# Two weighted sums at a time, and the feed-forward's token sums and second plain unit moved into the end of the attention

## The chip, the cores and the metric

The kernel runs on one core of a Trainium2 chip. The metric is the time of one execution in device microseconds (us). Engines are named as in the profile: PE multiplies matrices, DVE does vector arithmetic, ACT activations, casts and copies, POOL the rest of the vector work, SP issues most transfers. PSUM, the memory that PE writes, has eight banks of 512 fp32 values per partition.

## What is computed

One transformer block on 2048 tokens of width 640, in fp32:

```python
h  = x + attention(layernorm(x)) @ wo          # 32 heads of 20, a token sees itself and 255 before it
h2 = h + (gelu(n @ w_gate) * (n @ w_up)) @ w_down   # n = layernorm(h), inner width 1536
```

## The kernel before

**Numbers.** Each fp32 operand of the dense products is held as two fp16 halves, high and low; a product is three matmuls (high with high, high with low, low with high). A split is a cast on ACT and a subtraction on DVE.

**Attention.** The tokens are 16 blocks of 128. A block has eight units of four heads; a unit looks at up to three blocks of keys. For each unit there are a maximum (`maxima`: products on PE, masking and reduction on DVE in `max_out`), the scores (`scores`: products again with the maximum folded in, the exponential on ACT and masking on POOL in `score_out`, result in a buffer `pt` of which there are three), and the weighted sum (`value_lane`: 12 matmuls `ps<-pt,v` into a bank, copied by ACT to `oT` in `value_out`). `row_lane` issues maxima and scores two units at a time, one in each of two sets of three banks; below, such a group of 24 matmuls is a ROW, and 12 matmuls of a weighted sum are a VAL. A ROW can start when the two sets are free: one waits for DVE's reduction, the other for ACT's exponential. After four units `normalise` transposes `oT` and divides; after eight, `o_transpose` splits the block and turns it through transposing DMAs (or, for the last block, on PE), and `wo_block` multiplies it with `wo` (weights w3h, w3l). Keys lie in a ring `kT` of three slots of two blocks. Key and query projections (`qk`, weights w0 and w1) and values (`vproj`, w2) are dense products that the lane `dense_lane` hands out 15 matmuls at a time between the ROWs.

**Feed-forward.** The tokens are four chunks of 512, the inner width three groups of 512; a unit (chunk, group) is a `gate_up`, then a `down` of 96 matmuls (DN). Units go in the order `SEQ` (L1165): (0,0), (1,0), (0,1), (1,1), ... Units (0,0) and (1,0) have a plain `gate_up` (L1364): 120 matmuls of 512 columns in eight groups of 15 (PLAIN). All others use a scheme with fewer products (`gate_up_sums`, L1228: twice 108 matmuls of 256 columns, SUMS), which needs sums of token blocks (`token_sums`, L1317: ten additions and four splits per chunk, tiles tTh and tTl) and sums of weight blocks (class `Sums`, L488; `sums`, L524: four additions into a tile `sums`, of which one is in use at a time). Weights come through a ring of three stage slices `wsl`: once for their scale (`scale`: ACT squares each slice, a matmul with `dg` on PE makes the maximum known to all partitions) and once for the split.

**The order of work.** Everything is written by generators ("lanes"). A clock inside the kernel estimates when each engine is free and each operand ready, and a loop at the end (L1680 on) takes the first lane of a list that may start: ready outputs first, then transposes, side work, and PE's three lanes. Each engine's program is thus a fixed queue, and an instruction behind a waiting one waits too.

**Around the change.** When the projections are used up, `dense_lane` (L1548) opens the pool `ffb` and fills its turns with `first_feed_forward` (L1608): PLAIN and DN of unit (0,0). When all blocks are out it closes the attention's pools, opens `ffp` in their room and goes on with (1,0). The token sums of chunks 0 and 1, the second loading of the group-1 weights and the splits of these weights all follow that opening.

Of the kernel before, what the change touches and what calls it, by code (L numbers as in the profile page):

```python
# [23 lines left out]
P = 128  # L24
# [240 lines left out]
def block_kernel(ctx: ExitStack, tc: tile.TileContext, x, wqkv, wo, wg, wu, wd, out):  # L265
# [115 lines left out]
    class Weight:  # L381
# [19 lines left out]
        def load(self, room):  # L401
            self.sliced = False
            for i in range(self.shape[0]):
# [4 lines left out]
        def load_slices(self, turn):  # L408
            self.sliced = True
            for i in self.order if turn else range(self.shape[0]):  # L410
# [75 lines left out]
    class Sums(Weight):  # L486
# [3 lines left out]
        N = 17  # L490

# [21 lines left out]
        def rest(self, hi, lo, src, sc, name, i):  # L513
# [3 lines left out]
            opened["sums"] -= name[0] in ("S", "EE")  # L517
            if i is not None:
                self.left[i] -= 1
                if not self.left[i]:  # L520
                    for _ in range(2 if i < 2 else 1):
                        self.done_with()
# [13 lines left out]
        def split(self, hl):  # L536
            self.hl = hl
            self.left, self.tm = {0: 3, 1: 3, 2: 2}, {}
# [11 lines left out]
            yield on("vector", e, when=lambda: opened["sums"] < 1)  # L550
            t = nc.tile(ffp, [P, 4, 256], F32, "sums")
            opened["sums"] += 1
            nc.vector.tensor_tensor(t[:, 0], e[:, :256], e[:, 256:], op=ALU.subtract)
            yield from self.take(16, t[:, 0], ("EE", 0), 2)
# [156 lines left out]
    kT = wp.tile([P, RK // 2, H // 2, CW], F16, name="kT")  # L711
# [373 lines left out]

    def value_out(j, u, ps):
        b = B[j]
        yield on("scalar", ps[:, 0:P], when=lambda: u == 0 or b.kept == u)
        if u % 4 == 0:
            b.oT = at("oT", [P, 4, P], F32, 1)  # L1090
        nc.scalar.copy(b.oT[:, u % 4, :], ps[:, 0:P])
        done(ps)
        b.kept = u + 1
        if u % 4 == 3:
            tps.append(normalise(j, u // 4, b.oT))

    def normalise(j, half, oT):
# [6 lines left out]
        for u4 in range(4):  # L1104
            nc.tensor.transpose(t[:, u4 * P:u4 * P + OR], oT[:OR, u4, :], ident[:OR, :OR])
        tv = t.rearrange("p (h e) -> p h e", e=32)
# [60 lines left out]
    POOL = (0, 1, 1, 0)  # L1167
    ffpools = [None, None]
# [21 lines left out]
    def gate_out(c, fg, ft, pss):  # L1190

        i = SEQ.index((c, fg)) % 2
# [34 lines left out]

    def gate_up_sums(c, fg):  # L1228
        i = SEQ.index((c, fg)) % 2
# [3 lines left out]
        ah = nc.tile(ffpools[i], [P, FT, CB * P], F16, "ah")  # L1233
        al = nc.tile(ffpools[i], [P, FT, CB * P], F16, "al")
# [82 lines left out]
    def token_sums(c):  # L1317

        yield on("vector", when=lambda: ffpools[1] and chunk[c] == CB
                 and (c == 0 or ("T", c - 1) in flags))  # L1320
        pool = ffpools[1 - POOL[c]]
        tT[c] = tuple(nc.tile(pool, [P, 8, 256], F16, n) for n in ("tTh", "tTl"))
# [5 lines left out]
        x = nc.tile(ffp, [P, 4, 256], F32, "tsum")  # L1328
# [431 lines left out]
```

## Time and profile before

| what | value |
| --- | --- |
| median of 3 runs (lowest, highest) | 1029.72 us (1029.27, 1033.44) |
| the profiled execution: its time, its span | 1026.79 us, 1025.1 us |
| busy, share of the span | PE 94%, DVE 71%, ACT 47%, POOL 23% |
| mean granted clock of PE | 0.99 |
| chain that ended last, by engine | PE 72%, DMA 9%, DVE 8%, ACT 4%, issue 4%, POOL 2% |

The span runs from the first to the last instruction of the profiled execution. A row of the timeline gives start, duration, engine, operation and count; a bracket at its end gives the idle time of the engine just before it and what ended it. Nearly all rows have line L211, a helper through which every instruction is issued, so places are found by tile names and time. A VAL's 12 matmuls are fp32 and leave 24 records. Pieces overlap on PE, so the length of one is taken from its start to the start of the next. A row of the table of stretches gives the stretch and its length, busy time and count of PE, PEld (PE's weight load), DVE, ACT and POOL, then PE's granted clock, the DMA engines' busy share and GB/s.

### The profile page before, as it was taken

The page shows a single profiled execution, that of the slowest core. Times are in us where ns is not written, and L with a number is a line of the kernel's source. Part 1 is how long each engine was busy: PE and PEld are TensorE (multiplying, and loading weights), DVE is VectorE, ACT ScalarE, POOL GpSimd, SP SyncE. Part 2 cuts the span into 40 slices and gives each one's busy share as a digit, 9 for nine tenths or more (in the row PEclk, how much of TensorE's full clock was granted, in tenths as well). Part 3 has the DMA queues.
Part 4 walks back from the last instruction along what each step waited for, and adds up shares of the span by engine and source line. Part 5 has one row for each costly group of instructions (what it writes and reads, how often), then busy time and mean ns, then how long its engine had stood idle before and what let it go on. Part 6 is the DMA issues. An engine that isn't in the chain of part 4 may idle for free.

```text
span 1025.1 us, 27364 instructions
## 1 busy us (share of the span) xinstructions
PE 960.0 (94%) x11687; PEld 730.9 (71%) x11687; DVE 732.6 (71%) x1393; ACT 478.6 (47%) x769; POOL 240.4 (23%) x336
## 2 busy tenths in 40 slices
PE   3997898999899999998989889989999999999998
PEld 2885675767677867776556655878888888888886
DVE  6978886767866656666878338979978869764563
ACT  6635664555556655555665635453522224231120
POOL 5202233544434333333334420000121100000000
PEclk9999999999999999999989999999999999999999
DMA  8447675463463613517474214252443322100002
GB/s 333 124 126 208 176 186 127 92 130 85 88 148 76 138 47 92 106 40 206 137 163 80 41 42 143 80 155 78 110 98 100 94 91 72 40 14 1 1 1 103
DMA packets 109306, 106.90 MB, mean 104 GB/s; under 512 B 59136, under 2 KB 79872, under 8 KB 107264
## 3 DMA queue, kind: packets, MB, share of 16 engines
q1 hardware_dynamic: 86080, 94.40, 35.1%
q10 hardware_dynamic: 23104, 10.75, 4.1%
q8 instruction: 91, 1.49, 0.6%
q14 instruction: 31, 0.25, 0.1%
HBM read 71.11 MB, written 20.97 MB: 90 GB/s over the span
## 4 chain that ended last, share of the span: by engine, by line
PE 72%; DMA 9%; DVE 8%; ACT 4%; issue 4%; POOL 2%; ACTq 1%; SPq 0%; DVEq 0%; POOLq 0%
PE ps L211 72%; DMA ol<-spl 2%; DMA xt<-in_x_dram 2%; ACT pt L211 2%; DMA qk<-qks 2%; DVE mxs L211 1%; DMA wsl<-in_wd_dram 1%; DVE gel L211 1%; DMA h0l<-spl 1%; POOL pt L211 1%; POOL spl L211 1%; ACTq L211 1%; DVE ps L211 1%; DVE tsum L211 1%; ACT wsl L211 1%
## 5 line engine op out<-in xcount | busy, mean ns | idle before, releaser
L211 ACT ACTIVATE pt<-ps,esc 128x1536 f32<-128x1536 f32 (+2 forms) x128 | 186.4, 1460 | 97.8 <-PE ps L211 87.9
L211 POOL TENSOR_SCALAR_AFFINE_SELECT pt<-pt 128x512 f32<-128x512 f32 x240 | 151.4, 653 | 265.8 <-ACT pt L211 265.6
L211 DVE TENSOR_REDUCE mxs<-ps 128x4 f32<-128x1024 f32 (+1 forms) x128 | 151.4, 1186 | 2.7
L211 DVE TENSOR_TENSOR gel<-gel,ps 128x512 f32<-128x512 f32 x140 | 93.9, 683 | 52.7 <-PE ps L211 52.2
L211 DVE COPY_PREDICATED ps<-mask,ps 128x512 f32<-128x512 int32 x112 | 77.4, 692 | 64.2 <-PE ps L211 63.6
L211 PEld LDWEIGHTS <-wu 128*128 128x128 f16 x1080 | 105.7, 98 | 12.2
L211 PEld LDWEIGHTS <-gu 128*128 128x128 f16 x888 | 86.6, 98 | 36.4 <-issue 2.9
L211 PE MATMUL ps<-pt,v 128*21 128x128 f32 x2880 | 106.0, 277 | 5.9 <-ACT pt L211 2.5
L211 PE MATMUL ps<-qT,kT 62*128 62x128 f16 x1440 | 101.1, 219 | 5.1 <-ACT pt L211 2.4
L211 PEld LDWEIGHTS <-qT 60*128 60x128 f16 x1440 | 80.3, 94 | 35.2 <-issue 34.9
L211 PE MATMUL ps<-kT,qT 60*128 60x128 f16 x1440 | 102.7, 218 | 2.6 <-DVE mxs L211 1.8
L211 PEld LDWEIGHTS <-ah 128*128 128x128 f16 x768 | 74.7, 98 | 31.3 <-issue 3.1
L211 PEld LDWEIGHTS ps<-pt,v 128*21 128x21 f32 x2880 | 68.2, 101 | 26.3 <-POOL pt L211 5.2
L211 DVE SCALAR_TENSOR_TENSOR ht<-ps,ffk,ht 128x320 f32<-128x320 f32 x96 | 52.1, 546 | 43.7 <-PE ps L211 43.2
L211 PEld LDWEIGHTS <-kT 62*128 62x128 f16 x1440 | 78.7, 95 | 6.1 <-issue 5.2
L211 PE MATMUL ps<-wdh,ah 128*128 128x320 f16 x256 | 76.6, 299 | 2.1 <-ACT oT L211 1.4
L211 PE MATMUL ps<-wdh,al 128*128 128x320 f16 x256 | 76.5, 299 | 0.0
L211 PE MATMUL ps<-wdl,ah 128*128 128x320 f16 x256 | 76.5, 299 | 0.0
L211 ACT CAST ah<-gel 128x512 f16<-128x512 f32 x48 | 29.6, 617 | 95.6 <-DVE gel L211 95.5
L211 PE MATMUL ps<-xh,w0h 128*128 128x256 f16 x200 | 55.7, 279 | 8.8 <-ACT w0h L211 5.4
L211 PE MATMUL ps<-tTh,wu 128*128 128x256 f16 x320 | 60.6, 273 | 0.0
L211 PE MATMUL ps<-xh,w1h 128*128 128x256 f16 x200 | 54.5, 274 | 4.0 <-ACT oT L211 3.4
(219 smaller groups left out, 2273.8 us busy)
## 6 DMA issues: line engine op xcount, KB each, us to landing
wsl<-in_wd_dram SPq DMA_DIRECT2D x28, 320.0 KB
qk<-qks ACTq DMA_DIRECT2D x64, 128.0 KB
wsl<-in_wg_dram SPq DMA_DIRECT2D x30, 256.0 KB
wsl<-in_wu_dram SPq DMA_DIRECT2D x30, 256.0 KB
qT<-qk SPq DMA_DIRECT2D x16, 320.0 KB
kT<-qk SPq DMA_DIRECT2D x16, 320.0 KB
ht<-in_x_dram SPq DMA_DIRECT2D x16, 320.0 KB
h_dram<-ht SPq DMA_DIRECT2D x16, 320.0 KB
```

Source lines behind the costliest of these rows:

```text
L211: r = real(*args, **kw)
```

## The change

1. The weighted sums take two units at once: `value_lane` waits until two units are in its queue and issues their 24 matmuls back to back into one bank, and `value_out` copies both with one ACT copy.
2. The plain `gate_up` of unit (1,0) is issued inside the attention, behind unit (0,0). Its gelu is the tanh-approximation activation, where (0,0) builds its own from tanh. What follows the attention is the DN of (1,0), then SUMS of (0,1) and (1,1).
3. The token sums of chunks 1 and 0 are issued inside the attention too, with the x tiles as room for intermediates; the attention ends only when those of chunk 0 are done. Chunk 0's result lies in the third slot of the key ring, which moves to a pool that outlives the attention.
4. The second slot of that ring gives two buffers for sums (`KSUM`, handed out by `sum_room`), the first one the activations of every other unit (`act_room`).
5. Three slices of the group-1 gate weights are loaded again before the attention ends; the other two, and those of the up weights, after it. Chunk 1's `ht` tiles are loaded right at the end of the attention.
6. The loop's list of outputs puts `max_out` and `score_out` ahead of other outputs.

```diff
         def sums(self, k):
+            yield on("vector", when=lambda: idle_sums and (1, k) in self.raw
+                     and (1, k + 2) in self.raw)
             a, b = self.raw[1, k], self.raw[1, k + 2]
             a1, a2, b1, b2 = a[:, :256], a[:, 256:], b[:, :256], b[:, 256:]
-            yield on("vector", a, b, when=lambda: opened["sums"] < 1)
-            t = nc.tile(ffp, [P, 4, 256], F32, "sums")
-            opened["sums"] += 1
+            yield on("vector", a, b, when=lambda: idle_sums)
+            t, _ = sum_room(self, ("S", k))
...
-                tasks.append(self.sums(k))
+                tasks.append(self.sums(1) if not k else self.end_sum())
...
-    kT = wp.tile([P, RK // 2, H // 2, CW], F16, name="kT")
+    kT = ffw.tile([P, RK // 2, H // 2, CW], F16, name="kT")
+    kparts = [kT[:, i, 8 * k:8 * k + 8, :] for i in range(3) for k in range(2)]
+    KAH, KSUM, KTOK = 0, 2, 4
+    idle_sums = [KSUM, KSUM + 1]
+
+    def sum_room(w=None, name=None):
+        i = idle_sums.pop(0)
+        if w:
+            w.at_[name] = i
+        return kparts[i].bitcast(F32).rearrange("p (a b) n -> p a (b n)", b=2), i
...
-            yield pe(when=lambda: valq and B[valq[0][0]].v == 2 and pos["ones"])
-            j, u = valq.popleft()
+            yield pe(when=lambda: len(valq) > 1 and B[valq[0][0]].v == 2 and pos["ones"])
+            units = sorted(valq.popleft() for _ in range(2))
+            j = units[0][0]
             b = B[j]
-            pt = b.pt.pop(u)
+            pts = [b.pt.pop(u) for _, u in units]
             ks = window(j)
             n = len(ks)
             order = [1, 0, 2] if n == 3 else list(range(n))
-            yield pe(pt[:, 3 - n:3], slots=["pv"])
+            yield pe(*(pt[:, 3 - n:3] for pt in pts), slots=["pv"])
             ps = bank("pv")
-            pv = ps[:, 0:P]
-            for k, i in enumerate(order):
-                for c in range(4):
-                    nc.tensor.matmul(pv[32 * c:32 * c + DH + 1],
-                                     vring[ks[i] % RV][:, 4 * u + c, :], pt[:, 3 - n + i, c, :],
-                                     start=(k == 0), stop=(k == n - 1))
-            pos["values"] += 1
-            tasks.append(value_out(j, u, ps))
-            if u == 7:
+            for m, (_, u) in enumerate(units):
+                pv = ps[:, m * P:m * P + P]
+                for k, i in enumerate(order):
+                    for c in range(4):
+                        nc.tensor.matmul(pv[32 * c:32 * c + DH + 1],
+                                         vring[ks[i] % RV][:, 4 * u + c, :],
+                                         pts[m][:, 3 - n + i, c, :],
+                                         start=(k == 0), stop=(k == n - 1))
+                pos["values"] += 1
+            tasks.append(value_out(j, [u for _, u in units], ps))
+            if pos["values"] % (H // 4) == 0:
...
-        yield on("scalar", ps[:, 0:P], when=lambda: u == 0 or b.kept == u)
-        if u % 4 == 0:
+        yield on("scalar", ps[:, 0:2 * P], when=lambda: pos["norm"] == 2 * j + us[0] // 4)
+        if b.kept % 4 == 0:
             b.oT = at("oT", [P, 4, P], F32, 1)
-        nc.scalar.copy(b.oT[:, u % 4, :], ps[:, 0:P])
+        x, y = (u % 4 for u in us)
+        nc.scalar.copy(b.oT[:, x:y + 1:y - x, :], ps[:, 0:2 * P].rearrange("p (a q) -> p a q", q=P))
         done(ps)
-        b.kept = u + 1
-        if u % 4 == 3:
-            tps.append(normalise(j, u // 4, b.oT))
+        b.kept += 2
...
+    def act_room(i):
+        if i:
+            return [t.rearrange("p (a b) n -> p a (b n)", b=2) for t in kparts[KAH:KAH + 2]]
+        return [nc.tile(ffpools[0], [P, FT, CB * P], F16, n) for n in ("ah", "al")]
...
-        yield on("vector", when=lambda: ffpools[1] and chunk[c] == CB
-                 and (c == 0 or ("T", c - 1) in flags))
+        last = ("T", (1, None, 0, 2)[c])
+        yield on("vector", when=lambda: chunk[c] == CB and (c == 1 or last in flags)
+                 and (c or B[NB - 3].scored))
         pool = ffpools[1 - POOL[c]]
-        tT[c] = tuple(nc.tile(pool, [P, 8, 256], F16, n) for n in ("tTh", "tTl"))
+        tT[c] = (kparts[KTOK:KTOK + 2] if POOL[c] == 0 else
+                 tuple(nc.tile(pool, [P, 8, 256], F16, n) for n in ("tTh", "tTl")))
...
+        if c < 2:
+            o, q = (at("xt", [P, D], F32)[:, :512].rearrange("p (a n) -> p a n", a=2)
+                    for _ in range(2))
+        else:
+            yield on("vector", when=lambda: idle_sums)
+            x, taken = sum_room()
+            o, q = x[:, 0:2], x[:, 2:4]
...
+        yield from W["g", 1].load_slices(1, (0, 2, 1))
         yield ("sync",), need(when=lambda: ffpools[1] and W["d", 1].scaled, eng="sync")
         room = nc.tile(ffp, [P, 2, 17 * 256], F16, "wu2").bitcast(F32)
         room = room.rearrange("p a f -> p (a f)")
-        W["g", 1].load([room[:, 512 * k:512 * k + 512] for k in range(KC)])
-        W["u", 1].load([nc.tile(ffp, [P, D], F32, "ht", CB)[:, :512] if k < CB else
-                        room[:, 512 * KC:512 * KC + 512] for k in range(KC)])
+        W["g", 1].load({k: room[:, 512 * k:512 * k + 512] for k in (3, 4)})
+        W["g", 1].sliced, W["g", 1].ring = True, (0, 2, 1)
+        W["u", 1].load([room[:, 512 * (KC + k):512 * (KC + k) + 512] if k < 3 else
+                        nc.tile(ffp, [P, D], F32, "lxn", 2)[:, :512] for k in range(KC)])
...
-        while pos["h"] < NB or any(not b.wrote for b in B):
+        while pos["h"] < NB or any(not b.wrote for b in B) or ("T", 0) not in flags:
...
-                    side.extend(((LATE, chunk_lane(0)), (LATE, norm_lane(1, range(CB), "h"))))
+                    side.extend(((LATE, chunk_lane(0)), (LATE, norm_lane(1, range(CB), "h")),
+                                 (LATE, token_sums(1)), (LATE, token_sums(0))))
...
-        side.append((LATE, token_sums(0)))
+        load_h(1, ffp, CB)
         for c in range(1, NCH):
-            if c == 1:
-                side.append((LATE, after_lane(lambda: W["u", 1].ready, token_sums(1))))
-            side.append((LATE, chunk_lane(c)))
+            if c > 1:
+                side.append((LATE, chunk_lane(c)))
...
         yield from gate_up(0, 0)
         yield from down(0, 0)
+        yield from gate_up(1, 0)
 
     def feed_forward():
+        yield from down(*SEQ[1])
         prev = None
-        for c, fg in SEQ[1:]:
+        for c, fg in SEQ[2:]:
...
+        outs.sort(key=lambda l: l.gen.__name__ not in ("max_out", "score_out"))
```

PE, in the middle of the attention, before: the last matmul of a dense group, one VAL (pt is the unit's exponentials, v0 to v5 the values), the first weight load of a ROW.

```order
L211 MATMUL ps8_73<-xh_3908,w0l_219 128x256
L211 MATMUL ps8_73<-pt_5274,v0_101 21x128 x4
L211 MATMUL ps8_73<-pt_5274,v5_106 21x128 x4
L211 MATMUL ps8_73<-pt_5274,v1_102 21x128 x4
L211 LDWEIGHTS qT_4441
```

The same place now, with two units:

```order
L211 MATMUL ps8_73<-pt_5171,v0_101 21x128 x4
L211 MATMUL ps8_73<-pt_5171,v5_106 21x128 x4
L211 MATMUL ps8_73<-pt_5171,v1_102 21x128 x4
L211 MATMUL ps8_73<-pt_5245,v0_101 21x128 x4
L211 MATMUL ps8_73<-pt_5245,v5_106 21x128 x4
L211 MATMUL ps8_73<-pt_5245,v1_102 21x128 x4
L211 LDWEIGHTS qT_4435
```

The work is the same, in half as many groups: 64 in the whole program, where there were 124.

ACT, at the end of the attention, before (pt: an exponential; oT: the copy of a weighted sum; sph, oh: the high halves of a block's result):

```order
L211 CAST sph_9372<-o32_9195 128x640
L211 ACTIVATE pt_9375<-ps8_73,esc_109 128x1536
L211 ACTIVATE pt_9376<-ps8_73,esc_109 128x1536
L211 COPY oT_9448<-ps8_73 128x128
L211 ACTIVATE pt_9422<-ps8_73,esc_109 128x1536
L211 ACTIVATE pt_9423<-ps8_73,esc_109 128x1536
```

The same place now (gel: the gelu of unit (1,0); kT: token sums in the key ring):

```order
L211 ACT_TABLE_LOAD
L211 ACTIVATE gel_9323<-ps8_73,ffk_85 128x512
L211 COPY oT_9211<-ps8_73 128x256
L211 ACT_TABLE_LOAD
L211 ACTIVATE pt_9353<-ps8_73,esc_109 128x1536
L211 ACTIVATE pt_9354<-ps8_73,esc_109 128x1536
L211 CAST sph_9406<-o32_9135 128x640
L211 CAST kT_107<-xt_9349 128x512
L211 CAST kT_107<-xt_9348 128x512
L211 CAST ah_9299<-gel_9323 128x512
L211 ACT_TABLE_LOAD
```

ACT's program has seven table loads behind the first instruction's, where it had one, and the cast of a block's result stands behind two exponentials instead of ahead of them.

SP, where the attention ends, before (h_dram: the blocks of h; wu2: raw weights):

```order
L211 DMA h_dram_72<-ht_8777 128x640
L211 DMA h_dram_72<-ht_9327 128x640
L211 DMA wu2_9710<-in_wg_dram 128x512 x5
L211 DMA ht_9716<-in_wu_dram 128x512
```

And now:

```order
L211 DMA h_dram_72<-ht_8629 128x640
L211 DMA h_dram_72<-ht_9218 128x640
L211 DMA ht_9835<-h_dram_72 128x640
L211 DMA ht_9837<-h_dram_72 128x640
L211 DMA ht_9839<-h_dram_72 128x640
L211 DMA ht_9841<-h_dram_72 128x640
L211 DMA wu2_9847<-in_wg_dram 128x512 x2
L211 DMA wu2_9847<-in_wu_dram 128x512 x3
```

Four loads of chunk 1 now stand ahead of the group-1 weights, of which two gate slices are left.

## Rows read from the trace of the kernel before

**Rows 1.** Table of stretches.
```profile
300.00:460.00 160.00, 156.79 (x2666) 118.17 (x2668) 100.86 (x137) 87.20 (x119) 59.77 (x89) 1.00 0.37 83
460.00:575.00 115.00, 103.83 (x1558) 66.94 (x1559) 88.87 (x178) 71.62 (x118) 43.91 (x60) 0.97 0.54 136
575.00:611.00 36.00, 29.45 (x439) 18.55 (x429) 5.34 (x12) 19.82 (x26) 13.61 (x21) 0.91 0.13 23
...
692.00:1025.10 333.10, 329.70 (x2786) 272.33 (x2784) 237.83 (x441) 90.58 (x140) 18.27 (x16) 1.00 0.22 62
```

**Rows 2.** Timeline of PE: a VAL, a ROW, a dense group; two VALs together.
```profile
283.18 0.85 PE L211 MATMUL ps<-pt,v 128*21 128x128 f32 x24
283.97 0.23 PE L211 MATMUL ps<-kT,qT 60*128 60x128 f16 x1
...
284.74 0.28 PE L211 MATMUL ps<-xh,w1h 128*128 128x256 f16 x1
...
577.90 1.51 PE L211 MATMUL ps<-pt,v 128*21 128x128 f32 x48
579.34 0.83 PE L211 MATMUL ps<-ident,oT 117*128 117x117 f32 x4
```

**Rows 3.** Timeline of PE: the next ROW, the dense group behind it.
```profile
286.49 0.23 PE L211 MATMUL ps<-kT,qT 60*128 60x128 f16 x1
...
287.58 0.28 PE L211 MATMUL ps<-xh,w1h 128*128 128x256 f16 x1
```

**Rows 4.** Timeline of DVE between these two ROWs.
```profile
285.58 1.23 DVE L211 TENSOR_REDUCE mxs<-ps 128x4 f32<-128x1024 f32 x1
```

**Rows 5.** Timeline of PE: a ROW with only one VAL ahead of it.
```profile
462.55 0.21 PE L211 MATMUL ps<-qT,kT 62*128 62x128 f16 x1 [0.61 <-ACT pt L211]
```

**Rows 6.** Timeline of PE: the second block's last transposition, its product with wo.
```profile
145.19 0.62 PE L211 MATMUL ps<-ident,oT 117*128 117x117 f32 x4
...
159.22 0.45 PE L211 MATMUL ps<-w3h,ol 128*128 128x320 f16 x1 [2.91 <-DMA ol<-spl]
```

**Rows 7.** Timeline of PE, end of the attention: from the last VAL on.
```profile
602.00 0.77 PE L211 MATMUL ps<-ident,oT 117*128 117x117 f32 x4
...
605.50 0.34 PE L211 MATMUL ps<-w3h,ol 128*128 128x320 f16 x1 [0.28 <-DVE ol L211]
...
606.16 0.47 PE L211 MATMUL ps<-w3h,ol 128*128 128x320 f16 x1
606.43 0.47 PE L211 MATMUL ps<-w3h,oh 128*128 128x320 f16 x1
```

**Rows 8.** Timeline of ACT: two exponentials, the table load at the attention's end.
```profile
597.34 2.97 ACT L211 ACTIVATE pt<-ps,esc 128x1536 f32<-128x1536 f32 x2 [0.69 <-PE ps L211]
...
604.90 1.28 ACT L211 ACT_TABLE_LOAD   x1
```

**Rows 9.** Page, costliest groups: masks on POOL (us in all, mean ns).
```profile
L211 POOL TENSOR_SCALAR_AFFINE_SELECT pt<-pt 128x512 f32<-128x512 f32 x240 | 151.4, 653 | 265.8 <-ACT pt L211 265.6
```

**Rows 10.** Timeline of SP, then of ACT: gate weights loaded, their first split.
```profile
612.13 2.39 SPq L211 DMA_DIRECT2D wu<-in_wg_dram  x5
...
615.80 0.50 ACT L211 ACTIVATE wg<-wu,sw 128x256 f16<-128x256 f32 x1
```

**Rows 11.** Timelines of DVE and ACT: a weight sum, a cast and a low half of four.
```profile
618.13 0.42 DVE L211 TENSOR_TENSOR sums<-wu 128x256 f32<-128x256 f32 x1
...
621.51 1.15 ACT L211 ACTIVATE wg<-sums,sw 128x1024 f16<-128x1024 f32 x1
...
623.33 1.28 DVE L211 SCALAR_TENSOR_TENSOR wg<-sums,sw,wg 128x1024 f16<-128x1024 f32 x1
```

**Rows 12.** Timeline of PE: the scales of the group-2 weights.
```profile
676.13 0.49 PE L211 MATMUL ps<-dg,ones 128*128 128x128 f32 x2 [2.46 <-DVE dg L211]
676.45 0.27 PE L211 MATMUL ps<-h1h,wg 128*128 128x256 f16 x1
...
682.71 0.39 PE L211 MATMUL ps<-dg,ones 128*128 128x128 f32 x2
```

More of the change, by code (lines that the diff above doesn't have):

```diff
@@ L402, in load @@
             self.sliced = False
-            for i in range(self.shape[0]):
+            for i in room if isinstance(room, dict) else range(self.shape[0]):
                 nc.sync.dma_start(room[i], self.src[:, i, :])
@@ L406, in load, with load_slices @@
             self.loaded = True
-        def load_slices(self, turn):
+        def load_slices(self, turn, some=None):
             self.sliced = True
-            for i in self.order if turn else range(self.shape[0]):
+            for i in some or (self.order if turn else range(self.shape[0])):
                 yield ("sync",), need(when=lambda: pos["taken"] < pos["used"] + SLICES, eng="sync")
@@ L490, in block_kernel @@
         N = 17
+        ring = range(KC)
         @property
@@ L516, in rest @@
             self.have.add(name)
-            opened["sums"] -= name[0] in ("S", "EE")
+            if name[0] in ("S", "EE"):
+                idle_sums.append(self.at_[name])
             if i is not None:
@@ L520, in rest @@
                 if not self.left[i]:
-                    for _ in range(2 if i < 2 else 1):
-                        self.done_with()
+                    for k in (i, i + 2) if i < 2 else (4,):
+                        pos["used"] += self.sliced and k in self.ring
         def sums(self, k):
+            yield on("vector", when=lambda: idle_sums and (1, k) in self.raw
+                     and (1, k + 2) in self.raw)
             a, b = self.raw[1, k], self.raw[1, k + 2]
             a1, a2, b1, b2 = a[:, :256], a[:, 256:], b[:, :256], b[:, 256:]
-            yield on("vector", a, b, when=lambda: opened["sums"] < 1)
-            t = nc.tile(ffp, [P, 4, 256], F32, "sums")
-            opened["sums"] += 1
+            yield on("vector", a, b, when=lambda: idle_sums)
+            t, _ = sum_room(self, ("S", k))
             for o, x, y, op in ((1, a2, b2, ALU.add), (0, t[:, 1], a1, ALU.subtract),
@@ L537, in split @@
             self.hl = hl
-            self.left, self.tm = {0: 3, 1: 3, 2: 2}, {}
+            self.left, self.tm, self.at_ = {0: 3, 1: 3, 2: 2}, {}, {}
+            tasks.append(self.sums(0))
             for k in range(2):
                 yield on("scalar", when=lambda: (1, k) in self.raw and (1, k + 2) in self.raw)
-                tasks.append(self.sums(k))
+                tasks.append(self.sums(1) if not k else self.end_sum())
                 b = self.raw[1, k + 2].rearrange("p (a f) -> p a f", a=2)
@@ L549, in split, with end_sum @@
             yield from self.take(slice(14, 16), e.rearrange("p (a f) -> p a f", a=2), ("E", 0), 2)
-            yield on("vector", e, when=lambda: opened["sums"] < 1)
-            t = nc.tile(ffp, [P, 4, 256], F32, "sums")
-            opened["sums"] += 1
+            yield on("scalar", when=lambda: 2 in self.tm)
+            yield from self.take(16, self.tm[2][:, 0], ("EE", 0), 2)
+        def end_sum(self):
+            yield on("vector", when=lambda: idle_sums and (1, 4) in self.raw)
+            e = self.raw[1, 4]
+            yield on("vector", e, when=lambda: idle_sums)
+            t, _ = sum_room(self, ("EE", 0))
             nc.vector.tensor_tensor(t[:, 0], e[:, :256], e[:, 256:], op=ALU.subtract)
-            yield from self.take(16, t[:, 0], ("EE", 0), 2)
+            self.tm[2] = t
     C_Q, C_K, C_V, C_WO, C_G, C_U, C_D = 0, 1, 2, 3, 4, 7, 10
@@ L1357, in token_sums @@
         yield from store(4, q)
+        if c > 1:
+            idle_sums.append(taken)
         flags.add(("T", c))
-    def after_lane(when, gen):
-        yield on("vector", when=when)
-        yield from gen
     def gate_up_plain(c, fg):
-        pool = ffpools[SEQ.index((c, fg)) % 2]
+        pool = ffpools[side_of(c, fg)]
         wg_, wu_ = W["g", fg], W["u", fg]
@@ L1429, in chunk_lane @@
     def chunk_lane(c):
-        yield ("sync",), need(when=lambda: (c == 0 or c == 1 and W["u", 1].ready
-                                            or c > 1 and chunk["out", 3 - c] == CB), eng="sync")
+        yield ("sync",), need(when=lambda: (c < 2 or c > 1 and chunk["out", 3 - c] == CB), eng="sync")
         load_h(c, ffpools[POOL[c]], CB)
@@ L1585, in dense_lane @@
                 else:
-                    yield pe(when=lambda: woq or all(b.wrote for b in B))
+                    yield pe(when=lambda: woq or all(b.wrote for b in B) and ("T", 0) in flags)
         nonlocal ffp
```

21 lines of the change are left out of this document (12 added, 9 removed).

## The prediction

> **What bounds the kernel now.** I read the page first: PE is busy for 94% of the span, so a change of order can only win in the rest and in stretches where PE ran slowly. The table of stretches says where these are [rows 1]. From 692 us on PE is busy for 329.70 of 333.10 us at full clock: nothing to win. From 300 to 460 us it is 156.79 of 160. Between 460 and 575 us 11.2 us are idle, between 575 and 611 us 6.6, at clocks of 0.97 and 0.91, and there is a stall at 676 us. I then took PE's timeline for the price of each piece, the waits for who ends its idle time, and the queues of ACT, DVE and SP for what stands behind each other. Both programs hold the same matmuls, so every term is a wait, a switch or a slow clock.
>
> **1. Two units at a time.** One VAL takes 0.79 us from its start to the next piece, two together take 1.44 [rows 2]. A merge saves 2 x 0.79 - 1.44 = 0.14 us; ROW (0.77) and dense groups keep their lengths. There are 124 groups before and 64 now, so 60 merges: **-8.1 us**. If half of that is lost at the neighbours, it is -4.
>
> **2. ROWs with less between them.** A ROW waits for the DVE reduction of the ROW before. In the piece shown it starts at 286.49, with only 15 query or key matmuls since the last one; the reduction ends at 285.58 + 1.23 = 286.81, and the ROW takes 1.09 us instead of 0.77 [rows 2 to 4]: a wait of 0.32. A VAL between them hides it. In the new order 12 pairs of ROWs (of three key blocks) have such a group alone between them, where there were 3: 9 x 0.32 = **+2.9 us**. On the other side three places go where one VAL and no dense group lay between ROWs; one of them shows 0.61 us of waiting for an exponential [rows 5], and I take that for all three: **-1.8 us**.
>
> **3. The second unit's wait.** A merged VAL needs both units' exponentials and masks: 1.5 us on ACT [rows 8], then two masks of 0.65 us on POOL [rows 9], 2.8 us. The later of the two units was issued at least a dense group and a ROW earlier (1.7 + 0.8 us), and its masked parts are used 0.9 us into the VAL. That just suffices, so the wait is between nothing and the 0.61 us of rows 5; it is nearer to nothing, as a margin is left. I take 0.05 us a pair, 60 x 0.05 = **+3.0 us**; the upper end, +37, is a rival below.
>
> **4. The products with wo.** The second block's waited 2.91 us for its transposed low half, which was there 14 us after the last transposition of oT [rows 6]. The new order puts about 12.5 us of PE work between the two: **-2.0 us** (0 to -3). Later blocks keep about their distance.
>
> **5. The end of the attention, 575 to 611 us.** At full clock the pieces there come to: 4 ROWs 3.1, 10 VALs 7.5, 60 matmuls with wo 8.6, a DN part 1.7, transpositions 1.8; together 22.7 of 36.0 us. The loss is **13.3 us**: waits for exponentials and masks, the serial end from the last VAL to wo (602.00 to 605.50), and matmuls at 0.27 us a piece, the 1.2 GHz level, where 2.4 GHz gives 0.135 [rows 7]. DVE is nearly empty there (5.3 us of 36), ACT half busy [rows 1]. With the change most of (1,0)'s 120 wide matmuls lie between the last ROWs, up to 30 at a time (6.5 us), longer than two exponentials (2.97) and a pair of masks, so these no longer stop PE. What stays: the serial end, 3.5 less 0.85 of work, 2.65; a slow clock after it, 1.5 (0 to 2); block 14's wo, 2.5; a transposition behind an oT copy behind a gelu, 1.0. The wait for wo is new, since the cast of that block's high half now stands behind a table load and two exponentials (1.28 + 2.97 us [rows 8]), with 9.3 us of PE work as cover where 8.3 sufficed: at most 3.2. Together 7.7: **-5.6 us** (-11 to 0).
>
> The token sums, two times ten additions and eight casts and subtractions at some 0.7 us (their tiles are twice the 0.42 us sums of rows 11), lie in DVE's and ACT's empty time there. Without that cover they stand between the weight sums on DVE, as they do now. The second sums buffer shortens nothing that PE waits for, so I give it nothing. ACT gets six more table loads, 1.28 us each [rows 8], 7.7 in all; I charge PE nothing for them beyond the above, as a load and two exponentials (4.3 us) still end inside 30 wide matmuls. The Trainium skill speaks against this: its page "ScalarE: Activation LUTs" ("What ACT_TABLE_LOAD costs", "Rules for kernel authors") wants all work of one table set done before switching and counts 2.66 us a switch, a drain included. The load in rows 8 shows 1.28 us, and no exponential follows it, so the drain can't be seen there; by the page the six would be an estimated 16 us of ACT time.
>
> **6. After the attention.** Before, 120 wide matmuls (26 us) covered the group-1 weights; now the DN of (1,0) does, 96 x 0.136 = 13.1 us. The first split follows the issue of the gate loads by 3.7 us [rows 10]. Three slices are there already. The other two queue behind four loads of h (some 3 us) and land about 8 us after wo ends; their sums (4 x 0.42), a cast (1.15) and a low half (1.28) [rows 11] end at 12.4 us, with four additions of DN on DVE between at 14.5. The second step of SUMS needs them at 13.1 + 1.3 = 14.4 us: just in time. The old order has a stall of 2.46 us for the scale of the group-2 weights, released by DVE, whose queue holds the token sums of chunk 1 there; behind it 43 matmuls of 256 columns took 6.26 us [rows 12], where 0.135 x 256 / 320 = 0.108 each makes 4.7. That is 4.0 us in all, and the token sums are gone from there. I keep 1.5 us for both places: **-2.5 us** (-4 to +6).
>
> **Sum.** -8.1 + 2.9 - 1.8 + 3.0 - 2.0 - 5.6 - 2.5 = -14.1 us. The profiled execution took 1026.79, so it would take 1012.7; the median of the runs shown is 2.9 above that execution, so I forecast a median of 1015.5.
>
> **The rivals.**
> *Late weights.* The group-1 weights come 5 us after DN ends, as DN's additions and the sums share DVE's queue, and the clock falls for another 1.5. For it: the margin above is zero. Against it: three slices are early, and two sums buffers let DVE run ahead. 1022.
> *Table loads on the path.* They push the exponentials beyond the cover and PE pays all six, 7.7 us: 1023. Against it: the cover of 6.5 us. By the page's 2.66 us PE would pay an estimated 16 us, and the change would give nothing.
> *The pair waits* (the slower side). Without term 3 the sum is -17.1 us. If each of the 60 merged VALs waits for its later unit by over 17.1 / 60 = 0.29 us, the change isn't faster; from 0.37 us it is slower by 5 us. At 0.5 us, near the 0.61 of rows 5, it comes to 1029.7 - 17.1 + 30 = 1043. Against it: before, a VAL followed its unit's ROW by about 3 us too, and PE was 98% busy from 300 to 460 us.
> *The gaps fill better.* No waits of terms 2 and 3 and none of the 5 us kept in term 5 for wo, oT and the clock: 1004.6.
>
> **How the numbers follow.** Forecast 1015.5, own range 1008 to 1022: 0.55. Late weights 0.13, table loads 0.13 (0.05 of it with the page's price), pair waits 0.09, better filling 0.10. The range reaches from 1004 to 1029 to hold the time 8 times in 10; it leaves out the pair waits and the outer parts of the others. A measurement of this kernel can tell about 0.5%, 5.1 us, from no change. Faster by more than that (below 1024.6) are the forecast, better filling and most of late weights and table loads: 0.80. Within 0.5%: 0.12. Slower: 0.08.
>
> **What would show it.** In the new profile: VALs of 48 records in 1.44 us with no idle time ahead of them (1; idle time ended by POOL or ACT pt there would be the pair's wait); ROWs of 1.09 us behind single groups (2); PE over 90% busy in the last 36 us of the attention, its idle time ended by ol, oT and the serial end (5); table loads of 1.28 us with ACT waiting, not PE (5); no idle time between the DN of (1,0) and the first SUMS, and no long wait on dg (6). The prediction is wrong if the stretch that is now 98% busy gets new idle time, or if the way from the last wo to the end, now 1025 - 611 = 414 us, doesn't shrink by the 26 us that moved and some 2.5 more.

## The result: 18 us faster, and the profile after

| | before | after |
| --- | --- | --- |
| median (lowest, highest), 4 runs each | 1029.49 us (1028.95, 1033.44) | 1011.45 us (1006.36, 1015.40) |
| ratio, 95% interval | | 0.9832 [0.9806, 0.9858] |
| profiled execution: time, span | 1026.79, 1025.1 us | 1011.27, 1009.6 us |
| last product with wo ends at | 611.0 us | 618.7 us |
| from there to the end | 414.1 us | 390.9 us |

The table of stretches of the changed kernel, with the attention's end from 575 us on, then the stretches behind the attention; the first three answer to those of [rows 1].

```profile
300.00:460.00 160.00, 157.07 (x2747) 120.95 (x2745) 102.14 (x144) 89.42 (x102) 62.23 (x93) 1.00 0.38 88
460.00:575.00 115.00, 109.19 (x1597) 72.68 (x1595) 95.24 (x192) 76.08 (x114) 43.18 (x59) 0.99 0.56 140
575.00:618.70 43.70, 41.63 (x443) 23.94 (x442) 17.57 (x29) 28.45 (x32) 12.05 (x17) 1.00 0.06 16
618.70:695.20 76.50, 74.48 (x633) 61.69 (x631) 67.16 (x140) 42.10 (x78) 0.00 (x0) 1.00 0.46 148
695.20:1009.60 314.40, 308.47 (x2594) 254.18 (x2591) 221.17 (x409) 81.70 (x126) 16.98 (x16) 0.99 0.22 60
```

The stretch from 300 to 460 us has kept its 98%. From 460 to 575 us PE's idle time went from 11.2 to 5.8 us; the end of the attention, which had 6.6 us idle at a clock of 0.91, has 2.1 us at full clock. The end now holds PLAIN of unit (1,0). PE's timeline there: a piece of PLAIN, a merged VAL, the ROW, the wo of block 14, later the transpositions and the wo of the last block.

```profile
581.09 0.38 PE L211 MATMUL ps<-h1h,gu 128*128 128x512 f16 x1
581.40 1.51 PE L211 MATMUL ps<-pt,v 128*21 128x128 f32 x48
583.00 0.85 PE L211 MATMUL ps<-qT,kT 62*128 62x128 f16 x24
...
584.55 0.31 PE L211 MATMUL ps<-w3h,ol 128*128 128x320 f16 x1 [0.32 <-DMA ol<-spl]
...
613.03 0.55 PE L211 MATMUL ps<-ident,o 128*128 128x128 f32 x3 [0.66 <-DVE o L211]
614.14 0.31 PE L211 MATMUL ps<-w3h,oh 128*128 128x320 f16 x1 [0.57 <-ACT oh L211]
614.29 0.30 PE L211 MATMUL ps<-w3l,oh 128*128 128x320 f16 x1
614.87 0.31 PE L211 MATMUL ps<-w3h,ol 128*128 128x320 f16 x1 [0.28 <-DVE ol L211]
615.01 0.30 PE L211 MATMUL ps<-w3h,oh 128*128 128x320 f16 x1
```

The VAL waits for nothing. Block 14's wo waits 0.32 us, where I had kept 2.5. The serial end is still there (0.66, 0.57 and 0.28 us of waits), but the matmuls behind it stay at 0.135 us, the 2.4 GHz level, where those in [rows 7] fell to 0.27.

Two places got worse. The first is early. ACT's, ACT's queue's and PE's timelines, at the first scores of a block, whose maxima (mT) ACT sends into qT:

```profile
73.25 0.24 ACT L211 COPY mT<-ps 64x128 f16<-64x128 f16 x1
73.52 1.94 ACTq L211 DMA_DIRECT2D qT<-mT  x2
81.11 0.26 PE L211 MATMUL ps<-qT,kT 62*128 62x128 f16 x1 [4.19 <-DMA qT<-mT]
...
149.78 1.29 ACTq L211 DMA_DIRECT2D qT<-mT  x2
153.38 0.29 PE L211 MATMUL ps<-qT,kT 62*128 62x128 f16 x1 [3.11 <-DMA qT<-mT]
```

The first of these two waits stands in the kernel before too, where PE's order is the same up to there; it is shorter, 1.32 us in the first profile of that kernel and 2.44 us in a second one (e12). PE's timeline before (first profile):

```profile
78.54 0.21 PE L211 MATMUL ps<-qT,kT 62*128 62x128 f16 x1 [1.32 <-DMA qT<-mT]
```

The second is in the feed-forward, at the start of unit (3,2), which had no idle time before. DVE's, ACT's and PE's timelines: kT is the room of chunk 3's token sums.

```profile
804.78 0.68 DVE L211 TENSOR_TENSOR kT<-kT,h0l 128x512 f32<-128x512 f32 x1
805.37 0.55 DVE L211 SCALAR_TENSOR_TENSOR ht<-ps,ffk,ht 128x320 f32<-128x320 f32 x1
...
811.52 0.62 ACT L211 CAST kT<-kT 128x512 f16<-128x512 f32 x1 [4.89 <-DVE kT L211]
...
812.19 0.27 PE L211 MATMUL ps<-kT,gu 128*128 128x256 f16 x1 [1.98 <-ACT kT L211]
812.91 2.65 PE L211 MATMUL ps<-kT,gu 128*128 128x256 f16 x17 [0.46 <-DVE kT L211]
```

PE waits 2.44 us here, matmuls behind it run at half clock, and the unit takes 28.2 us instead of 23.6.

**An account by pieces.** To compare kernels I sum what each piece on PE takes, from its start to the start of the next, beyond its price at full clock (ROW 0.78, a merged VAL 1.44, a single one 0.79, a matmul with wo 0.136, and so on), where it is over 0.25 us. "End" is the 45 us up to the last wo.

| us lost in | 0 to 90 | 90 to 300 | 300 to end | end | behind | sum |
| --- | --- | --- | --- | --- | --- | --- |
| before (first profile) | 19.1 | 21.6 | 19.3 | 12.9 | 4.5 | 77.3 |
| after (first profile) | 21.0 | 24.3 | 13.2 | 2.9 | 5.8 | 67.1 |
| before, again (e12) | 18.8 | 21.7 | 17.7 | 13.0 | 4.2 | 75.5 |
| pairs only (e1) | 19.3 | 21.9 | 13.1 | 19.8 | 4.9 | 79.0 |
| plain behind (e3) | 21.0 | 25.2 | 14.0 | 18.0 | 3.9 | 82.1 |
| after, again (e5) | 21.3 | 24.1 | 11.7 | 2.9 | 2.0 | 61.9 |
| scores later (e7) | 20.0 | 19.2 | 12.1 | 5.9 | 2.0 | 59.2 |
| sums behind (e8) | 19.6 | 21.9 | 12.2 | 4.3 | 22.8 | 80.8 |
| single units (e9) | 20.8 | 19.5 | 13.2 | 1.8 | 1.0 | 56.3 |

Kernels with pairs have 8.1 us less to begin with. With that the sums follow the spans to within 3 us.

### The profile page after: what moved, and what is told of

Same layout as the page of the kernel before. It is cut to its first block, busy times and chain, and to the rows that moved or that the text cites. A ratio compares the mean times of both kernels' runs of the same rounds, so it can differ in the third digit from the quotient of the medians.

```text
span 1009.6 us, 27335 instructions
## 1 busy us (share of the span) xinstructions
PE 953.7 (94%) x11687; PEld 737.4 (73%) x11687; DVE 730.7 (72%) x1393; ACT 484.1 (48%) x711; POOL 238.1 (24%) x336
## 4 chain that ended last, share of the span: by engine, by line
PE 54%; DVE 22%; DMA 10%; ACT 6%; issue 5%; POOL 2%; SPq 1%; ACTq 1%; DVEq 0%; POOLq 0%
PE ps L211 54%; DVE gel L211 4%; DVE mxs L211 3%; DVE kT L211 3%; DVE ps L211 2%; DMA lxn<-h_dram 2%; ACT pt L211 2%; DVE ht L211 2%; DMA qT<-mT 1%; DMA h0l<-spl 1%; ACT wsl L211 1%; DVE wu L211 1%; DMA wsl<-in_wd_dram 1%; DMA wsl<-in_wg_dram 1%; DVE gu L211 1%
## 5 line engine op out<-in xcount | busy, mean ns | idle before, releaser
L211 ACT ACTIVATE pt<-ps,esc 128x1536 f32<-128x1536 f32 (+2 forms) x128 | 186.4, 1460 | 77.3 <-PE ps L211 64.2
L211 PEld LDWEIGHTS <-kT 62*128 62x128 f16 (+1 forms) x1920 | 126.6, 96 | 33.9 <-issue 11.6
L211 DVE COPY_PREDICATED ps<-mask,ps 128x512 f32<-128x512 int32 x112 | 77.4, 692 | 81.7 <-PE ps L211 80.8
L211 PE MATMUL ps<-kT,qT 60*128 60x128 f16 x1440 | 106.2, 219 | 8.7 <-DVE mxs L211 6.5
L211 PE MATMUL ps<-pt,v 128*21 128x128 f32 x2880 | 92.3, 276 | 2.4 <-ACT mT L211 1.5
L211 PEld LDWEIGHTS ps<-pt,v 128*21 128x21 f32 x2880 | 74.2, 101 | 16.8 <-issue 7.4
L211 PE MATMUL ps<-xl,w0h 128*128 128x256 f16 x200 | 56.4, 282 | 0.0
L211 PE MATMUL ps<-xl,w1h 128*128 128x256 f16 x200 | 56.1, 282 | 0.0
L211 PEld LDWEIGHTS <-ah 128*128 128x128 f16 x448 | 43.5, 98 | 16.8 <-issue 0.2
L211 PE MATMUL ps<-xh,w1l 128*128 128x256 f16 x200 | 55.7, 281 | 0.0
L211 PE MATMUL ps<-xh,w0l 128*128 128x256 f16 x200 | 55.6, 282 | 0.0
L211 ACT ACTIVATE gel<-gel,ffk 128x512 f32<-128x512 f32 x40 | 28.6, 719 | 45.8 <-DVE gel L211 45.7
```

Source lines behind the costliest of these rows:

```text
L211: r = real(*args, **kw)
```

## The experiments

Twelve runs in three groups of four, each group on one chip. The kernel before had medians of 1025.74, 1026.21 and 1026.15 us in the three groups, so ratios are compared, not times.

| run | median, us | ratio to before [95%] |
| --- | --- | --- |
| e1 pairs only | 1023.11 | 0.9972 [0.9953, 0.9991] |
| e2 pairs and order of the list | 1024.22 | 0.9980 [0.9961, 0.9998] |
| e3 plain unit behind | 1025.80 | 1.0009 [0.9985, 1.0033] |
| e4 gelu from tanh again | 1008.34 | 0.9827 [0.9786, 0.9868] |
| e5 the changed kernel again | 1007.47 | 0.9833 [0.9799, 0.9868] |
| e6 chunk 3 early | 1008.22 | 0.9844 [0.9810, 0.9878] |
| e7 scores later | 1001.93 | 0.9778 [0.9748, 0.9807] |
| e8 token sums behind | 1033.09 | 1.0063 [1.0033, 1.0093] |
| e9 single units | 1007.10 | 0.9807 [0.9781, 0.9832] |
| e10 before, scores later | 1023.07 | 0.9983 [0.9964, 1.0002] |
| e11 one sums buffer | 1013.73 | 0.9867 [0.9845, 0.9889] |
| e12 before again | 1025.43 | 0.9988 [0.9969, 1.0006] |

### e1, e9 and e12: the pairs

e1 takes `value_lane`, `value_out` and the `norm` count of the change into the kernel before. e9 puts the old ones back into the changed kernel:

```diff
-            units = sorted(valq.popleft() for _ in range(2))
+            j, u = valq.popleft()
```

> The kernel before with the weighted sums two units at a time and nothing else. My theory (a merge saves 0.14 us, 60 of them 8.1 us, and about 3 us of that go to ROWs with less between them): 1022 to 1026 us, VALs of 48 records in 1.44 us with no idle time ahead of them. Rival (each pair waits for its later unit, and the whole change hid that elsewhere): 1029 us or more, with idle time ahead of the VALs. Second rival (the gain of the whole change lies in the end of the attention alone): 1028 to 1031 us without any wait at the VALs.

> The changed kernel with the weighted sums one unit at a time again. The order of the attention moves with it in other places too. My theory, from the pieces of the traces (64 groups in place of 124 save some 8 us, but ROWs, which then have less between them, give about as much back in waits for reductions, exponentials and the maxima's transfer): between 3 us faster and 5 us slower than the changed kernel; in the trace the VALs take some 8 us more and the ROWs some 8 us less in all. Rival (the pairs keep 6 us or more of their 8): 6 to 9 us slower than the changed kernel.

> The kernel before as it is, for a profile on the chip of the runs beside it: ratio 1.00. If the account by pieces holds from run to run, its VALs take 110 to 115 us in all and its ROWs 110 to 116 us, where the pairs alone had 95 and 124.

Groups of PE's instructions by form, with the idle time ahead of each group and what ended it: maxima (kT,qT), scores (qT,kT), weighted sums (pt,v). First the kernel before (e12), then pairs only (e1), then the changed kernel.

```profile
L211 PE MATMUL ps<-kT,qT 60*128 60x128 f16 x1440 | 103.0, 218 | 2.1 <-DVE mxs L211 1.5
L211 PE MATMUL ps<-qT,kT 62*128 62x128 f16 x1440 | 101.6, 220 | 6.8 <-DMA qT<-mT 3.9 <-ACT pt L211 2.4 <-DVE o L211 0.3
L211 PE MATMUL ps<-pt,v 128*21 128x128 f32 x2880 | 106.3, 277 | 5.8 <-ACT pt L211 2.5 <-POOL pt L211 1.8 <-DVE gel L211 0.4
```

```profile
L211 PE MATMUL ps<-kT,qT 60*128 60x128 f16 x1440 | 103.3, 217 | 14.9 <-DVE mxs L211 9.0 <-DVE ps L211 2.3 <-DVE o L211 1.3
L211 PE MATMUL ps<-qT,kT 62*128 62x128 f16 x1440 | 100.8, 220 | 7.1 <-ACT pt L211 3.5 <-DMA qT<-mT 3.1
L211 PE MATMUL ps<-pt,v 128*21 128x128 f32 x2880 | 96.1, 279 | 6.7 <-ACT pt L211 4.1 <-POOL pt L211 1.5 <-DVE qks L211 0.6
```

```profile
L211 PE MATMUL ps<-kT,qT 60*128 60x128 f16 x1440 | 106.2, 219 | 8.7 <-DVE mxs L211 6.5 <-DVE lyax L211 0.5 <-DVE o L211 0.4
L211 PE MATMUL ps<-qT,kT 62*128 62x128 f16 x1440 | 102.6, 219 | 14.4 <-DMA qT<-mT 8.0 <-ACT pt L211 6.3
L211 PE MATMUL ps<-pt,v 128*21 128x128 f32 x2880 | 92.3, 276 | 2.4 <-ACT mT L211 1.5 <-DVE ht L211 0.8
```

The VALs are busy for 10 to 14 us less, and ahead of the end of the attention they wait no longer than before (1.0 us in e1, 1.9 in e12): a pair's wait does not show while there is other work. But the ROWs, which idled for 8.9 us in all, idle for 22.0 and 23.1 us. In e1 it is DVE's reductions (1.5 to 9.0 us) that PE now meets. Part comes back elsewhere: PE's waits for copies of oT fall from 9.8 us in 13 places to 3.6 in 6, and those for a block's low half ol from 5.9 to 1.3 us. And the end of the attention, with nothing to put between, loses 19.8 us in place of 13.0: there a pair does wait for both its exponentials, so my expectation of no idle time ahead of the VALs failed at this place. Net, e1 is 0.3% faster: 2.9 us (0.9 to 4.8), near the 4.0 that terms 1 to 3 gave together. Its 1023.1 us lie in the range I gave only because the kernel before took 1026 here and not 1030. e9 is the harder test, and my expectation of the time held: without the pairs the changed kernel is as fast (0.9807 against 0.9833, the intervals overlap). In its trace the ROWs idle for 15.3 us where e5 has 22.7, and by the account it has 4.6 us less from 90 to 300 us against the 8.1 that it pays at the VALs. Taken to the start of the next piece, its VALs come to 105 us against 89 in e5, 16 more where I expected some 8; that length also holds the waits of the pieces behind them. e12 repeats the account of the first profile of before to within 2 us. **In the kernel before the pairs are worth some 3 us, in the changed one nothing that shows; the result does not come from them.**

### e2, e7, e10: the order of the list, and scores behind their maxima

e2 adds the sorted list of outputs to e1. e7 and e10 count 2 us more from maxima to scores, in the changed kernel and in the one before:

```diff
+        outs.sort(key=lambda l: l.gen.__name__ not in ("max_out", "score_out"))
```

```diff
-        return nc.ready((B[j].c.qT[64 * par:64 * par + 62, prs[0], B[j].cols],), "tensor")
+        return nc.ready((B[j].c.qT[64 * par:64 * par + 62, prs[0], B[j].cols],), "tensor") + 2
```

> The kernel before with the pairs and with the list of outputs that puts max_out and score_out first. My theory (the order of the list moves only single waits): within 3 us of the pairs alone. Rival (the list is what thins out the waits for reductions and exponentials between 300 and 575 us, and what brought the new waits for the maxima's transfer at 81 and 153 us): over 4 us away from the pairs alone, with the waits on qT<-mT of 4.2 and 3.1 us there as after the whole change, and none without the list.

> The changed kernel, whose order counts 2 us more from the copy of the maxima to the first scores that use them. My theory (three scores stand too close behind the transfer qT<-mT, which takes 3.6 to 5.6 us from its copy, and PE loses 4.7, 0.6 and 4.0 us and then runs at half clock): no wait on qT<-mT of over 1 us, and 3 to 8 us faster than the changed kernel beside it. Rival (there is nothing else to do in the first blocks, so the wait moves to other pieces): the same or up to 5 us slower, with the idle time at 60 to 170 us ended by DVE mxs or ACT pt.

> The kernel before, whose order counts 2 us more from the copy of the maxima to the first scores that use them, as in the run of the changed kernel that gained by it. My theory (the short distance behind the maxima's transfer came with the pairs; the kernel before has one such wait, of 1.3 us at 77 us): within 3 us of the kernel before. Rival (the order of the first blocks was bad in both, and the repair has nothing to do with the change): 4 to 7 us faster than the kernel before.

e2 is 1.1 us from e1, so the list itself is worth nothing that shows. Pairs and list together set the order of the first blocks: e2 shares PE's order with the changed kernel up to the last projection, and the waits of the two ROWs are there too (2.71 us up to 79.58 us, ended by the transfer; 2.65 us up to 149.85 us, put down to DVE's o). The first of them needs no list: e1 has 2.54 us there. e7 is 5.5 us faster than the changed kernel in the same group (0.9778 against 0.9833), the best of all these kernels. Its waits for the maxima's transfer, then its stretch from 90 to 175 us, and the same stretch of the changed kernel:

```profile
PE ps L211 <- DMA qT<-mT: 1.0, 2, 0.7
```

```profile
90.00:175.00 85.00, 78.10 (x1096) 58.19 (x1095) 70.83 (x132) 51.98 (x89) 27.39 (x35) 1.00 0.70 167
```

```profile
90.00:175.00 85.00, 75.46 (x1061) 56.83 (x1060) 71.22 (x134) 49.94 (x85) 24.66 (x33) 0.96 0.71 171
```

The waits went from 8.0 to 1.0 us, and the clock in this stretch from 0.96 to 1.00; in the changed kernel the wait of 3.11 us in it had been followed by matmuls at half clock. The clock inside the kernel counts about 2.4 us from the copy to the landing; the rows above show 3.6 us from issue to use (149.78 to 153.38) and 7.6 (73.52 to 81.11). In the kernel before the same edit gains 1.7 us (0.9983, with an interval that takes in no change): it had the first of the two waits, and e10 has none there. The second belongs to the order that pairs and list make together, as neither e1 nor e9 waits for the transfer there. e7 beats both kernels, by 23 us the one and by 5.5 the other.

### e3: the second plain unit back behind the attention

```diff
         yield from down(0, 0)
-        yield from gate_up(1, 0)
...
+        yield from gate_up(*SEQ[1])
         yield from down(*SEQ[1])
```

> The changed kernel with the plain gate_up of unit (1,0) put back behind the attention; pairs, token sums inside the attention and the new rooms stay. My theory (PE lost 13 us at the end of the attention and the moved products fill that): 1020 to 1024 us, the last 36 us of the attention at 80 to 85% busy, with waits for exponentials and masks and a stall between the last weighted sum and the last wo. Rival (the moved unit only moves, the gain came from the token sums and the pairs): 1011 to 1014 us.

The whole gain is gone: 1.0009, 18 us behind the changed kernel (0.9833), and more than I expected: 1025.8 us is above my 1020 to 1024, and PE is busy for 76% of the last 36 us, not 80 to 85. Its end of the attention in the table of stretches, then waits of merged VALs in PE's timeline:

```profile
575.00:611.00 36.00, 27.29 (x350) 16.30 (x349) 16.73 (x28) 17.72 (x21) 13.91 (x17) 0.86 0.09 27
```

```profile
570.91 0.42 PE L211 MATMUL ps<-pt,v 128*21 128x128 f32 x8 [0.29 <-POOL pt L211]
...
573.38 0.42 PE L211 MATMUL ps<-pt,v 128*21 128x128 f32 x8 [0.62 <-POOL pt L211]
...
576.26 0.42 PE L211 MATMUL ps<-pt,v 128*21 128x128 f32 x8 [1.14 <-ACT pt L211]
577.51 0.42 PE L211 MATMUL ps<-pt,v 128*21 128x128 f32 x8 [0.82 <-POOL pt L211]
```

Here the pair waits are real, for exponentials and for masks. The end loses 18.0 us against 2.9 with the moved unit, 15.1 us, and from there to 700 us it loses 3.9 (waits on ah and am in the DN) against 0.8: together 18.2, which is what the ratios give.

### e8: the token sums back behind the attention

```diff
-        yield on("vector", when=lambda: chunk[c] == CB and (c == 1 or last in flags)
-                 and (c or B[NB - 3].scored))
+        yield on("vector", when=lambda: ffpools[1] and chunk[c] == CB and (c == 0 or last in flags))
...
+        side.extend(((LATE, token_sums(0)), (LATE, token_sums(1))))
```

> The changed kernel with the token sums of chunks 0 and 1 back behind the attention, in the room of a weight sum; the second plain unit stays in the gaps. My theory (the second unit can only move if the token sums move with it, since the DN of 13 us that is left behind the attention does not cover them): PE idles before the SUMS of unit (0,1) for 6 to 20 us, released by DVE or ACT, and the kernel is 8 to 24 us slower than the changed one. Rival (DVE is free enough behind the attention): within 3 us of it.

24 us slower than the changed kernel by the ratios, at my upper bound. The profiled execution was the shortest of ten (1023.1 us) and shows less than that: PE's timeline in the SUMS of (0,1), its waits alone.

```profile
632.73 0.37 PE L211 MATMUL ps<-kT,wg 128*128 128x256 f16 x1 [3.75 <-ACT kT L211]
...
635.00 2.51 PE L211 MATMUL ps<-kT,wg 128*128 128x256 f16 x11 [1.89 <-DVE kT L211]
...
643.87 0.27 PE L211 MATMUL ps<-kT,wg 128*128 128x256 f16 x1 [3.84 <-ACT kT L211]
...
645.74 3.48 PE L211 MATMUL ps<-kT,wg 128*128 128x256 f16 x17 [1.60 <-DVE kT L211]
...
672.48 0.79 PE L211 MATMUL ps<-dg,ones 128*128 128x128 f32 x2 [6.23 <-DVE dg L211]
```

The unit's 220 records stretch over 45.0 us and lose 21.0. The largest wait is the last, ahead of a product with dg (the scale of weights still to come), and DVE ends it. The edit also gives these token sums one of the two buffers for sums, which by e11 can cost about 1.2 us. Without the token sums the moved unit gains nothing (1.0063).

### e4: the table loads

```diff
-        yield from gelu(gel, pss[0], fg, pool, (c, fg) == (0, 0))
+        yield from gelu(gel, pss[0], fg, pool, fg == 0 and c < 2)
```

> The changed kernel with the gelu of unit (1,0) built from tanh, as that of (0,0) is: no table loads between the exponentials of the attention's end, but two more activations and three more DVE operations for each of the four gelus. My theory (the six table loads end inside the cover of the wide matmuls): 1010 to 1014 us, no change that can be measured. Rival (PE pays the table loads by way of the exponentials): 1003 to 1005 us (7.7 us less).

Six table loads fewer, and no difference: 0.9827 against 0.9833. By the intervals the 7.7 us of the rival would show, 3 us would not. ACT's timeline of the changed kernel shows a switch there and back:

```profile
580.33 0.63 ACT L211 CAST ah<-gel 128x512 f16<-128x512 f32 x1
580.97 1.28 ACT L211 ACT_TABLE_LOAD   x1
582.26 0.69 ACT L211 ACTIVATE gel<-ps,ffk 128x512 f32<-128x512 f32 x1
...
583.91 1.28 ACT L211 ACT_TABLE_LOAD   x1 [0.51 <-PE ps L211]
585.21 2.97 ACT L211 ACTIVATE pt<-ps,esc 128x1536 f32<-128x1536 f32 x2
```

A switch costs 1.29 us from the load's start to the next activation. The Trainium skill counts 2.66 us ("ScalarE: Activation LUTs", "What ACT_TABLE_LOAD costs"); its load of 1.28 us agrees, its drain is not there in these rows.

### e5, e6: the stall before unit (3,2)

e5 is the changed kernel once more. e6 lets the layernorm of chunk 3 and the token sums of chunks 2 and 3 be issued earlier:

```diff
-                side.extend((LATE, norm_lane(c, bs, n)) for bs, n in (((0, 2), "h"), ((1, 3), "i")))
-                side.append((LATE, token_sums(c)))
+                side.extend((1.5 if c == 3 else LATE, norm_lane(c, bs, n)) for bs, n in (((0, 2), "h"), ((1, 3), "i")))
+                side.append((1.5 if c == 3 else 1.5, token_sums(c)))
...
-                back = FFBACK.get(name, OUT)
+                back = max(FFBACK.get(name, OUT), self.back)
```

> The changed kernel as it is, as the yardstick for the runs beside it and for how often the stall of 2.0 us behind the casts of the token sums of chunk 3 (at 805 us, with 4.7 us lost) comes back. If it is a matter of the order of the queues it stands in this profile too, and the kernel takes 0.982 to 0.985 of the time of the kernel before.

> The changed kernel with layernorm and token sums of chunks 2 and 3 issued further ahead of their engines' other work. My theory (chunk 3's token sums stand 5 to 9 us later against their unit than before, behind additions of the units on DVE, and PE waits for their casts): the stall before unit (3,2) is gone, GUs there take 23.6 us instead of 28.2, and the kernel is 3 to 5 us faster than the changed one beside it. Rival (DVE and ACT have no room there, the additions that PE's banks wait for come later instead): no gain, and new idle time on PE between 690 and 800 us ended by DVE.

The stall is a matter of order: e5 has it, e6 has not (23.6 us for the unit, nothing lost from 690 us on). But its size was an accident of one execution. In e5 PE waited less, and the clock stayed:

```profile
807.91 0.27 PE L211 MATMUL ps<-kT,gu 128*128 128x256 f16 x1 [0.75 <-ACT kT L211]
808.64 2.02 PE L211 MATMUL ps<-kT,gu 128*128 128x256 f16 x17 [0.46 <-DVE kT L211]
```

1.2 us are lost there, not 4.7, and the median of e6 is no better (0.9844 against 0.9833). My 3 to 5 us were wrong: I took one profile's loss for the typical one.

### e11: one buffer for sums

```diff
-    idle_sums = [KSUM, KSUM + 1]
+    idle_sums = [KSUM]
```

> The changed kernel with one buffer for the sums of weight blocks and of tokens, as before, in place of two. My theory (the second buffer shortens nothing that PE waits for): within 2 us of the changed kernel, no idle time before the first SUMS unit. Rival (without it the group-1 weights come too late for 13 us of DN as cover, which is the case of the late weights): PE idles 2 to 5 us for the sums in the first SUMS unit, at 632 us, or at the next weights, and the kernel is 3 to 7 us slower.

By the medians I was wrong: 6 us slower than e5, or 3.5 us by the ratios (0.9867 against 0.9833), whose intervals overlap. The trace doesn't give these to the buffer. The order of every engine in the two kernels is the same past the last product with wo. The last transpositions of oT in PE's timelines of e6, e5, the first profile and e11, all with this order:

```profile
608.96 0.98 PE L211 MATMUL ps<-ident,oT 117*128 117x117 f32 x4
```

```profile
609.27 0.98 PE L211 MATMUL ps<-ident,oT 117*128 117x117 f32 x4
```

```profile
611.17 0.98 PE L211 MATMUL ps<-ident,oT 117*128 117x117 f32 x4
```

```profile
614.88 0.98 PE L211 MATMUL ps<-ident,oT 117*128 117x117 f32 x4
```

e11 had lost 5.6 us against e5 before anything differed. Behind that point, the first two SUMS lose 2.0 us against 0.8: about 1.2 us that one buffer can have cost. Why its four runs (1011.28 to 1014.16 us) all lie above those of e5 stays open; they lie inside the first four of the changed kernel (1006.36 to 1015.40 us).

## Why the prediction was right

The median came out 4 us below the forecast, and inside the own range of the likeliest case. But two large terms were wrong in opposite directions, and that their errors nearly cancel is luck. (Two products in the working are slightly off: 60 merges at 0.14 us are 8.4 us, not 8.1, and 60 matmuls with wo at 0.135 us are 8.1, not 8.6.)

- **Term 1** (-8.1) held in place: 48 records in 1.44 us.
- **Term 2** (+2.9 and -1.8) is the term that was mis-sized. The 12 ROWs behind a lone group are there, and 8 of them take 1.07 to 1.09 us as foretold, but the other four 1.67 to 3.48. In all, the idle time ahead of ROWs rose by 14.2 us, from 8.9 in e12 to 23.1 (22.7 in e5), most of it between 90 and 300 us (3.7 to 15 us), a stretch that [rows 1] leaves out. I had counted only the waits for the reduction of the ROW before. These rose from 1.5 to 6.5 us, and a faster PE also catches up with the maxima's transfer (3.9 to 8.0 us, part of it in a wait that was there before) and with exponentials (2.4 to 6.3 us).
- **Term 3** (+3.0) was nothing in the changed kernel. The pair waits of the slower rival are real only where PE has no other work, as e1 and e3 show at the end of the attention.
- **Term 4** (-2.0) held: the product of [rows 6] waits for nothing now. A second such wait, 3.2 us up to 520.21 us in e12, went too, which I hadn't counted; in all, waits for ol fell from 5.9 to 0.3 us.
- **Term 5** (-5.6) was too small. From e3 the moved unit gives 15.1 us at the end and 3.1 behind it. I measured the gain from the kernel before, which lost 13, but with pairs that end would lose 18 to 20 (e1, e3), and I kept 7.7 us where 2.9 stay: 2.5 of the serial end, as kept, 0.4 at block 14's wo in place of 2.5, and nothing of the slow clock and the oT copy.
- **Term 5, what I charged nothing for**: the table loads (e4) and the token sums (e8: free only under that cover) held. The second buffer is worth some 1.2 us in the trace; the medians say more, which the trace doesn't give to it (e11).
- **Term 6** (-2.5): SUMS of (0,1) starts without a wait, as forecast, the 2.46 us for the scale of the group-2 weights became 1.32 and 0.70 (1.10 in e5), and the way behind the attention loses 2.0 us (e5) against 4.2 (e12). The first profile had 5.8 there, since the token sums of chunk 3, which I hadn't followed, came too late. So the way from the last wo to the end shrank by 23.2 us, not by 26 and 2.5, and one of the prediction's own signs of being wrong came up; from e12 to e5 it is 27.1. The other did not: from 300 to 460 us PE is as busy as before.

In the ratios: pairs and list -2 us, token sums and rooms +3 (e3 against e2, whose intervals overlap), the moved unit -18. I had the first at -4.0 and the rest at -10.1. What the early gate slices and the early loads of chunk 1 are worth by themselves, no run shows.

## What to carry over

When a piece of work on the bounding engine gets shorter, ask of every wait in its stretch what it will now reach too early, and not only of the nearest one. Work moved into a gap is worth the gap that the rest of the change leaves there, which can be wider than the one in the profile of before. A stall seen in one execution has the size of that execution: look at a second profile before repairing it.

## What the runs showed of the hardware

- The same two transfers of 8 KB (qT<-mT) made PE wait 4.19, 4.73, 2.20 and 4.58 us at the same place of the same order (first profile, e5, e6, e11). The start of the last transposition of oT differs by 5.9 us among these four.
- Waits of 0.75 and 0.46 us in one unit left the clock alone (e5); 1.98 and 0.46 us at the same place were followed by matmuls at half clock, which cost another 2.2 us (first profile).
- A switch of ACT's table took 1.29 us, with no further gap ahead of the activation behind it.
